# Causal attention and a gated two-layer network on one core: every matmul with 128 columns of weights written as two of 64

## The chip, the cores and the metric

One NeuronCore of one Trainium2 chip (trn2) runs the whole kernel. The metric is device time of one execution in microseconds (us), on one core. PE is TensorE (matmuls; PEld is its weight loads), DVE is VectorE, ACT is ScalarE, POOL is GpSimd, and SP is the engine that issues the DMAs. [...]

## The reference

```python
# q, k, v: (4 batches, 12 heads, 448 positions, 64)   w_in: 768 x 2048   w_out: 2048 x 768
scores = (q @ k^T) / sqrt(64);  mask above the diagonal with -1e9
attn = exp(scores - rowmax);  attn = attn / (rowsum + 1e-9)
x = (attn @ v) as 1792 tokens x 768
h = x @ w_in
g = h * sigmoid(1.702 * h)
out = g @ w_out          # 1792 x 768, float32
```

The result has to be close to float32, so most operands are held as a pair of float16 tensors, a high part and a rest, and each product is three matmuls: high by high, high by rest, rest by high. The first attention batch does its scores in float32 instead. The weights arrive as 64-bit words and are rebuilt as float32 on chip.

## The kernel before, in words

**Tiling.** Each batch of 448 positions is cut into two blocks, of 256 and of 192 positions, so there are eight blocks. In a block, heads go two at a time; one such pair of heads is a *unit* (six per block, 48 in all). The work on PE comes in kinds:

- `turn` (matmul on line 870) transposes float32 q and k by an identity, two matmuls of 64 weight columns at a time (first batch only).
- `scores_of` makes scores: in the first batch `scores32` (line 1060), one float32 matmul with 128 weight columns per 64 queries of two heads; otherwise `scores` (line 1068), float16, where the two heads are two matmuls of 64 weight columns that write partitions 0 to 63 and 64 to 127 of one PSUM tile.
- `pv` in `unit` (line 1197) multiplies probabilities by v, also as pairs of 64 columns, 12 pairs in a unit of the 192-wide blocks (nine of them with 192 moving columns, three with 64).
- `h_slice` (line 1268) is x by w_in: 2304 matmuls with 128 columns of weights, 256 or 192 moving columns, nine to a step of the order. I call it H below.
- `out_tile` (line 1333) is g by w_out, 384 moving columns, six to a step; I call it O. Its weights are 128 columns of `gT`. The ring `gT` has seven places of 64 tokens, so in two of the 14 token tiles the 128 columns lie apart, and there the kernel already uses pairs of 64 (`takes`).
- `gram` (line 621, the columns' products of a piece of weights or v, 128 by 128, for a bound on its size) and `all_max` (line 430, one maximum brought to all partitions) are small matmuls with 128 columns.

In this text a matmul with 64 columns of weights is *narrow*, one with 128 is *wide*; two narrow ones that follow each other on the two halves of the array are a *pair*.

**What sets the order of the work.** Nothing is issued in program order. Each step is put on a list with `Ops.add` (costs per engine, what it reads and writes, a priority, how long its DMA takes, and whether its matmuls are narrow). `Ops.order` then searches: `forward` lays the steps out on the five engines by priority, `backward` makes new priorities from that layout, `late` scores a layout, and the best of 300 rounds is issued. In this ordering clock a change between narrow and wide on PE costs `SWITCH`, and `forward` has two PE queues, `PE` and `PE64`: it stays with the kind it has unless the other kind is ahead in priority by more than `keep`, drawn from `KEEP` for each round:

```python
SWITCH = 0.093
same, other = (ready["PE64"], q) if mode else (q, ready["PE64"])
q = same if same and (not other or same[0][0] <= other[0][0] + keep) else other
```

A DMA in the ordering clock starts `DMA_START` after its issue, holds the bus for its `dma`, and lands `DMA_END` later; transposes take `ROWS` for each 128 rows.

Of the kernel before, what the change touches and what calls it, by code (L numbers as in the profile page):

```python
# [59 lines left out]
class Ops:  # L60
# [11 lines left out]
    LOAD = 0.68  # L72
    DMA_START, DMA_END, DMA_DEPTH = 1.0, 0.8, 8
    ROWS = 0.19

# [8 lines left out]

    def add(self, costs, fn, r=(), w=(), prio=0.0, dma=0.0, narrow=False):
        deps = set()
        for key in r:
            if key in self.wrote:
                deps.add(self.wrote[key])
        for key in w:  # L90
            if key in self.wrote:
                deps.add(self.wrote[key])
            deps.update(self.read.get(key, ()))
        me = len(self.ops)
        for key in r:
            self.read.setdefault(key, []).append(me)
        for key in w:
            self.wrote[key] = me
            self.read[key] = []
        deps.discard(me)  # L100
        self.ops.append((costs, fn, sorted(deps), prio, dma, narrow))

    ROUNDS, STEPS, SPREAD, KEEP = 300, 6, (0.0, 0.0, 1.0, 3.0, 8.0), (0.0, 1.5, 4.0)

    SWITCH = 0.093

    def order(self):
        rnd = Random(SEED)
        best = now = self.scored([o[3] for o in self.ops], 0.0)
        bad = 0  # L110
        for _ in range(self.ROUNDS):
            spread = rnd.choice(self.SPREAD)
            now = self.scored(self.backward(now, spread, rnd), rnd.choice(self.KEEP))
# [9 lines left out]
    def scored(self, prios, keep):  # L123

        result, fin, last = self.forward(prios, keep)
        return 0.5 * last + sum(0.25 * self.late(result, Random(x)) for x in (1, 2)), result, fin

    def late(self, result, rnd):
        free = dict.fromkeys(self.ENGINES, 0.0)
        end = [0.0] * len(self.ops)  # L130
        bus, flying, clock, mode = 0.0, [], Clock(), False
        for i, e in result:
            costs, _, deps, _, dma, narrow = self.ops[i]
            start = max([free[e]] + [end[d] + self.HOP for d in deps])
            if e == "SP":
                start = max([start] + flying[-self.DMA_DEPTH :][: len(flying) // self.DMA_DEPTH][:1])
                free[e] = start + costs[e]
                bus = max(bus, start + self.DMA_START) + dma
                end[i] = bus + self.DMA_END + 0.8 * rnd.random()
                flying.append(end[i])  # L140
                continue
            if e == "PE":
                end[i] = clock.after(start, costs[e] + (self.SWITCH if narrow != mode else 0.0))
                mode = narrow
            else:
                end[i] = start + costs[e] * (1 + 0.03 * rnd.random()) + (0.15 * rnd.random() if e == "POOL" else 0.0)
            free[e] = end[i]
        return max(free.values())

    def backward(self, found, spread, rnd):  # L150
        _, result, fin = found
# [12 lines left out]
        while done < n:  # L164
# [4 lines left out]
            for e in self.ENGINES:  # L169
                if free[e] > now + 1e-9 or not ready[e]:  # L170
                    continue
                _, i = heappop(ready[e])
                costs, _, deps, _, dma, _ = self.ops[i]
                left[i] = free[e] = now + costs[e]
# [17 lines left out]

    def forward(self, prios, keep):

# [3 lines left out]
        for i, o in enumerate(self.ops):  # L198
            for d in o[2]:
                after[d].append(i)  # L200
        ready = {e: [] for e in self.ENGINES + ("BULK", "PE64")}
        mode = False
        coming = [(0.0, i) for i in range(n) if not wait[i]]
        taken = [None] * n
        free = dict.fromkeys(self.ENGINES + ("BULK", "PE64"), 0.0)
        bus = 0.0
# [5 lines left out]
        while len(result) < n:  # L212
            while coming and coming[0][0] <= now + 1e-9:
                _, i = heappop(coming)
                for e in self.ops[i][0]:
                    late = self.SECOND if e != next(iter(self.ops[i][0])) else 0.0
                    kind = "BULK" if e == "SP" and self.ops[i][4] > 1.0 else "PE64" if self.ops[i][5] else e
                    heappush(ready[kind], (prios[i] + late, i))
            moved = False
            free["BULK"] = max(free["SP"], bus - TUNE["slack"])  # L220
            for e in ("BULK",) + self.ENGINES:
                q = ready[e]
                if e == "PE":
                    same, other = (ready["PE64"], q) if mode else (q, ready["PE64"])
                    q = same if same and (not other or same[0][0] <= other[0][0] + keep) else other
                while q and taken[q[0][1]] is not None:
# [6 lines left out]
                e = "SP" if e == "BULK" else e  # L233
                costs, _, _, _, dma, narrow = self.ops[i]
                taken[i] = e
                free[e] = end = now + costs[e]
                if e == "PE":
                    end = clock.after(now, costs[e] + (self.SWITCH if narrow != mode else 0.0))
                    free[e] = free["PE64"] = end
                    mode = narrow  # L240
                if e == "SP":
# [80 lines left out]
def kernel(  # L322
# [9 lines left out]
    nc = tc.nc  # L332
# [79 lines left out]
    def flip(e, dst, src):  # L412
# [3 lines left out]
        )  # L416

    def all_max(src, src_key, tag, turn, prio):

# [5 lines left out]
        else:  # L425
# [3 lines left out]
            {"PE": 0.1},  # L429
            lambda e: nc.tensor.matmul(row, top, one16, start=True, stop=True),  # L430
            [src_key, "one16"], row_keys, prio,
# [181 lines left out]
    def gram(x, keys, ps, ps_key, first, last, prio):  # L613
# [5 lines left out]
        def mm(e):  # L619
            for k, m in blocks:  # L620
                nc.tensor.matmul(
                    ps[:, :P], t[:, k, m], t[:, k, m],
                    start=first and (k, m) == blocks[0],
                    stop=last and (k, m) == blocks[-1],
                )
# [148 lines left out]
    def v_batch(b, prio):  # L774
        st = bst[b]
        for j in range(NJ):
# [5 lines left out]
                ),  # L782
                [], [("vraw", j, 0)] + ([("vraw", j, 1)] if r == P else []), prio, dma=2.18 * r / P,
            )
# [77 lines left out]
    def turn(src, r, keys, prio):  # L862
# [10 lines left out]

        add({"PE": 2 * (4 * r / 2.4 + 210) / 1e3}, mm, keys + ident_keys, [("T", h)], prio, narrow=True)
        return ps_t[:, 256 * h : 256 * h + 2 * r].rearrange("p (t x) -> p x t", t=2), ("T", h)

    def k_unit32(u, c0, c1, prio):
# [5 lines left out]
        keys = [("q16", m, j) for j in range(4)]  # L883
        load_heads(f, k[0, 2 * u : 2 * u + 2, 64 * c0 : 64 * c1], r, [keys[:2], keys[2:]], prio, 0.045 * (c1 - c0))
        got, got_key = turn(f, r, keys, prio)
# [8 lines left out]
    def q_unit32(n, u, prio):  # L894
# [5 lines left out]
        keys = [("qf", i, j) for j in range(2)]  # L900
        load_heads(f, q[b, 2 * u : 2 * u + 2, 64 * c0 : 64 * c1], r, [[x] for x in keys], prio, 0.045 * ni)
        got, got_key = turn(f, r, keys, prio)
# [65 lines left out]
    def q_pair(n, u, prio):  # L968
# [7 lines left out]
        for a in range(2):  # L976
            for j in range(2):
# [6 lines left out]
                    ),  # L984
                    [], keys[-1:], prio, dma=0.09 * ni,
                )
# [61 lines left out]
    def scores_of(n, u, run, qt, qt_key, prio):  # L1048
# [9 lines left out]
        def scores32(e):  # L1058
            for i, ps in zip(run, places):
                nc.tensor.matmul(  # L1060
                    ps, qt[:, i - c0].rearrange("p j w -> p (j w)"), kt[:, : 64 * (i + 1)], start=True, stop=True
                )

# [14 lines left out]
        else:  # L1078
            add(
                {"PE": 2 * (o / 2.4 + 17 * len(run)) / 1e3}, scores, [qt_key] + kt_keys, bank(sb), prio, narrow=True  # L1080
            )
# [52 lines left out]
    def unit(n, u, prio):  # L1134
# [59 lines left out]
        def pv(e):  # L1194
# [11 lines left out]
            {"PE": sum((64 * (c1 - t[1]) / 2.4 + 5) for t in terms) / 1e3}, pv, v_keys + all_keys, [("PV", vb)], prio,  # L1206
            narrow=True,
        )
# [45 lines left out]
    def h_slice(n, sl, prio):  # L1254
# [7 lines left out]
        for t in range(2):  # L1262
            for a in range(0, NU, half):

                def mm(e, a=a, t=t):
                    for u in range(a, a + half):
                        for gw, gx in ((0, 0), (0, 1), (1, 0)):
                            nc.tensor.matmul(  # L1268
                                ph[:, t],
                                wib[:, sl, u, gw, t * P : (t + 1) * P],  # L1270
                                xT[x][:, gx, u, :w],
                                start=(u == 0 and gw + gx == 0),
                                stop=(u == NU - 1 and gw == 1),
                            )
# [32 lines left out]
    def out_tile(tt, prio):  # L1307
# [4 lines left out]

        takes = [(rs[0], P, 0)] if rs[1] == rs[0] + 1 else [(r, 64, 64 * j) for j, r in enumerate(rs)]
        for nh in range(2):
# [12 lines left out]
            for f0 in range(0, NFC, 2):  # L1327

                def mm(e, f0=f0, po=po, nh=nh):
                    for f in range(f0, f0 + 2):  # L1330
                        for gg, gw in ((0, 0), (0, 1), (1, 0)):
                            for r, m, o in takes:
                                nc.tensor.matmul(  # L1333
                                    po[o : o + m, :OH],
                                    gT[:, f, gg, 64 * r : 64 * r + m],
                                    wo_pair(f, gw, nh),
# [8 lines left out]
                    + [("gT", r, f, g) for f in (f0, f0 + 1) for g in range(2) for r in rs],  # L1345
                    [("O", pb)] + ([] if pb else [("T", 0), ("T", 1)]), 1e6 + prio, narrow=len(takes) > 1,
                )
# [114 lines left out]
```

## Time and profile before

| what | value |
|---|---|
| median of 3 runs | 640.23 us |
| the three runs | 640.47, 640.23, 637.7 us |
| span of the profiled execution, first to last instruction | 633.9 us |
| own time of the profiled execution | not listed apart; its span is 6.3 us under the median, 3.8 us under the fastest run |
| PE busy | 582.6 us, 92% of the span, 5723 matmuls |
| DVE busy | 422.4 us, 67% |
| ACT busy | 357.2 us, 56% |
| POOL busy | 96.6 us, 15% |

The slices of the span matter more than the totals: the share of an engine over the whole kernel is a mean over a start, in which weights and inputs arrive and are rebuilt, and a long rest. Matmuls are pipelined: a row's mean duration (246 to 327 ns) is that of one matmul from entry to modelled end, and their spacing, which is what one costs in a row of them, is read from how long a run of them took by the timeline or the chain.

### The profile page before, as it was taken

The numbers are of one execution on the slowest core, as the hardware profiler recorded it, in microseconds if no ns is written. First come the engines' busy times: TensorE is split into PE (matmuls) and PEld (weight loads), VectorE is DVE, ScalarE is ACT, GpSimd is POOL, SyncE is SP. The second block draws the span as 40 slices with busy tenths as digits, with TensorE's granted clock in tenths as the row PEclk, the third lists the DMA queues.
The fourth block names the chain that finished last, engine by engine and source line by source line (L and its number), as shares of the span: only waits on it lengthen the run. The fifth ranks groups of instructions, "written<-read, shape, count | busy, mean of one in ns | idle before, by whom it ended". The sixth has DMA issues, their size and how long they took to land. (4 is left out here: it accounts for less than half of the span.)

```text
span 633.9 us, 14759 instructions
## 1 busy us (share of the span) xinstructions
PE 582.6 (92%) x5723; PEld 439.5 (69%) x5723; DVE 422.4 (67%) x1128; ACT 357.2 (56%) x835; POOL 96.6 (15%) x235
## 2 busy tenths in 40 slices
PE   4777688978999999998999999999999999999997
PEld 3555466754588767876678667885679688777964
DVE  4999899999978898977498976769644213101300
ACT  4878888778657776758465565557343223012210
POOL 2233220043202124121021521001000000000000
PEclk9976689999999999999999999999999999999999
DMA  8999969678599687999847798627620040000000
GB/s 276 271 277 293 220 224 284 194 188 166 110 176 190 120 164 124 180 159 173 176 103 135 136 181 160 127 62 130 122 67 2 13 96 1 3 26 26 1 26 26
DMA packets 226407, 85.71 MB, mean 135 GB/s; under 512 B 207137, under 2 KB 216097, under 8 KB 226337
## 3 DMA queue, kind: packets, MB, share of 16 engines
q1 hardware_dynamic: 226336, 84.76, 62.7%
q8 instruction: 45, 0.74, 0.5%
q14 instruction: 26, 0.20, 0.1%
HBM read 41.68 MB, written 5.51 MB: 74 GB/s over the span
## 5 line engine op out<-in xcount | busy, mean ns | idle before, releaser
L1268 PE MATMUL ps_h<-xT,wib 128*128 128x192 f16 (+1 forms) x2304 | 239.3, 261 | 3.5 <-DVE gT L481 3.4
L1333 PE MATMUL ps_o<-wob,gT 128*128 128x384 f16 (+1 forms) x1536 | 233.8, 326 | 5.3 <-DVE wob L481 2.3
L1268 PEld LDWEIGHTS <-wib 128*128 128x128 f16 x2304 | 207.0, 98 | 31.8 <-issue 12.1
L1333 PEld LDWEIGHTS <-gT 128*128 128x128 f16 (+1 forms) x1536 | 131.4, 101 | 87.0 <-issue 12.6
L1105 ACT ACTIVATE z<-z,cols 128x320 f32<-128x320 f32 (+5 forms) x168 | 83.8, 500 | 47.1 <-DVE cols L1091 40.1
L1294 DVE SCALAR_TENSOR_TENSOR ps_h<-t,ps_h 128x512 f32<-128x512 f32 (+1 forms) x64 | 39.9, 624 | 76.5 <-ACT t L1289 76.3
L481 DVE SCALAR_TENSOR_TENSOR p<-z,cols,p 128x384 f16<-128x384 f32 (+3 forms) x168 | 82.6, 523 | 3.0 <-ACT p L476 1.9
L1091 DVE CUSTOM_DVE_ANT_0 z<-ps_s,mask,cols 128x384 f32<-128x384 f32 (+6 forms) x126 | 55.8, 478 | 30.1 <-PE ps_s L1068 30.1
L1289 ACT ACTIVATE t<-ps_h,cols 128x512 f32<-128x512 f32 (+1 forms) x64 | 40.1, 627 | 60.0 <-PE ps_h L1268 59.5
L476 ACT ACTIVATE p<-z,cols 128x128 f16<-128x128 f32 (+3 forms) x108 | 55.3, 538 | 15.4 <-DVE cols L1169 6.7
L1163 POOL TENSOR_SCALAR cols<-cols 128x2 f32<-128x2 f32 (+1 forms) x70 | 20.1, 287 | 208.6 <-ACT z L1105 207.7
L481 DVE SCALAR_TENSOR_TENSOR gT<-ps_h,gT 128x512 f16<-128x512 f32 (+1 forms) x64 | 39.6, 620 | 15.8 <-ACT gT L476 15.7
L476 ACT ACTIVATE gT<-ps_h 128x512 f16<-128x512 f32 (+1 forms) x58 | 31.1, 539 | 28.3 <-DVE ps_h L1294 28.1
L476 ACT ACTIVATE ob<-ps_o,cols 128x384 f32<-128x384 f32 x23 | 13.2, 575 | 59.8 <-PE ps_o L1333 59.8
L1197 PEld LDWEIGHTS <-v 128*64 128x64 f16 x864 | 38.4, 113 | 9.6 <-issue 7.6
L1197 PE MATMUL ps_v<-PT,v 128*64 128x192 f16 (+3 forms) x864 | 41.1, 243 | 4.1 <-DMA PT<-p 4.1
L1068 PE MATMUL ps_s<-kT,qT 128*64 128x192 f16 (+4 forms) x504 | 38.8, 277 | 2.4 <-DVE cols L1091 1.3
L1060 PE MATMUL ps_s<-kT,qT 128*128 128x64 f32 (+6 forms) x84 | 29.3, 468 | 2.6 <-DVE cols L1091 1.9
L1024 POOL TENSOR_SCALAR q<-q 128x512 f16<-128x512 f16 (+1 forms) x30 | 25.2, 841 | 43.0 <-ACT q L476 30.1
L1105 ACT ACTIVATION_READ_ACCUMULATOR z<-z,cols 128x1 f32 x168 | 31.7, 188 | 0.0
L476 ACT ACTIVATE wob<-wob 128x768 f32<-128x768 f32 (+1 forms) x19 | 20.8, 1095 | 15.6 <-DMA wob<-in_moe_w_in_dram 10.6
L1068 PEld LDWEIGHTS <-qT 128*64 128x64 f16 x504 | 19.6, 110 | 13.9 <-issue 9.9
(89 smaller groups left out, 541.1 us busy)
## 6 DMA issues: line engine op xcount, KB each, us to landing
wob<-in_moe_w_in_dram SPq DMA_DIRECT2D x16, 768.0 KB, 6.0
wob<-in_moe_w_out_dram SPq DMA_DIRECT2D x9, 768.0 KB, 5.5
vraw<-in_moe_w_out_dram SPq DMA_DIRECT2D x7, 768.0 KB, 5.4
out_dram<-ob SPq DMA_DIRECT2D x28, 192.0 KB, 2.1
vraw<-in_v_dram SPq DMA_DIRECT2D x12, 384.0 KB, 5.7
kf<-in_k_dram SPq DMA_DIRECT2D x36, 112.0 KB, 2.9
qf<-in_q_dram SPq DMA_DIRECT2D x48, 64.0 KB, 3.2
qf<-in_q_dram SPq DMA_DIRECT2D x48, 48.0 KB, 2.7
```

What stands on the lines that cost most here:

```text
L476: nc.scalar.activation(out=dst, in_=src, func=AF.Copy, scale=sc)
L481: nc.vector.scalar_tensor_tensor(out=dst, in0=src, scalar=sc, in1=hi, op0=ALU.mult, op1=ALU.subtract)
L1024: nc.gpsimd.tensor_scalar(out=dst, in0=src, scalar1=1.0, scalar2=1.0, op0=ALU.mult, op1=ALU.mult)
L1060: nc.tensor.matmul(ps, qt[:, i - c0].rearrange("p j w -> p (j w)"), kt[:, : 64 * (i + 1)], start=True, stop=True)
L1068: nc.tensor.matmul(ps[64 * j : 64 * j + 64], qt[:, g, i - c0, 64 * j : 64 * j + 64], kt[:, : i + 1, 64 * j : 64 * j + 64], start=(g == 0), ...
L1091: lambda e: nc.vector.tensor_tensor_reduce(out=z[:, :w], in0=ps, in1=mask[:, S - w :], scale=c, scalar=3.0e38, op0=ALU.add, op1=ALU.min, a ...
L1105: lambda e: nc.scalar.activation(out=z[:, :w], in_=z[:, :w], func=AF.Exp, bias=m, scale=-1.0, accum_out=l),
L1197: nc.tensor.matmul(ps[64 * j : 64 * j + 64, 64 * (first - c0) : w], vt[:, gv, J, j, :], PT[pi][:, at, gp, 64 * j : 64 * j + 64], start=(t ...
L1268: nc.tensor.matmul(ph[:, t], wib[:, sl, u, gw, t * P : (t + 1) * P], xT[x][:, gx, u, :w], start=(u == 0 and gw + gx == 0), stop=(u == NU - ...
L1289: lambda e: nc.scalar.activation(out=th, in_=ph, func=AF.Tanh, scale=ts[:, sl : sl + 1]),
L1294: lambda e: nc.vector.scalar_tensor_tensor(out=ph, in0=th, scalar=1.0, in1=ph, op0=ALU.add, op1=ALU.mult),
L1333: nc.tensor.matmul(po[o : o + m, :OH], gT[:, f, gg, 64 * r : 64 * r + m], wo_pair(f, gw, nh), start=(f == 0 and gg + gw == 0), stop=(f == ...
```

## The change

A helper `halves` issues a matmul with 128 weight columns as two with 64, for output partitions 0 to 63 and 64 to 127, with the same moving operand. `gram`, `all_max`, `scores32` and `h_slice` use it, and `out_tile` always takes its pairs of 64. So no matmul is wide any more. The flag `narrow`, the price `SWITCH`, the second PE queue and `keep` leave the ordering clock. Its DMA constants are set to other values: start 1.23 for 1.0, end 0.95 for 0.8, transposes 0.214 for 0.19 per 128 rows, and some loads' durations. The order is searched anew with these.

```diff
-    DMA_START, DMA_END, DMA_DEPTH = 1.0, 0.8, 8
-    ROWS = 0.19
+    DMA_START, DMA_END, DMA_DEPTH = 1.23, 0.95, 8
+    ROWS = 0.214
...
-    ROUNDS, STEPS, SPREAD, KEEP = 300, 6, (0.0, 0.0, 1.0, 3.0, 8.0), (0.0, 1.5, 4.0)
-
-    SWITCH = 0.093
+    ROUNDS, STEPS, SPREAD = 300, 6, (0.0, 0.0, 1.0, 3.0, 8.0)
...
-                if e == "PE":
-                    same, other = (ready["PE64"], q) if mode else (q, ready["PE64"])
-                    q = same if same and (not other or same[0][0] <= other[0][0] + keep) else other
...
+    def halves(out, lhsT, rhs, start, stop):
+
+        for o in range(0, P, 64):
+            nc.tensor.matmul(out[o : o + 64], lhsT[:, o : o + 64], rhs, start=start, stop=stop)
+
...
-                nc.tensor.matmul(
-                    ps, qt[:, i - c0].rearrange("p j w -> p (j w)"), kt[:, : 64 * (i + 1)], start=True, stop=True
-                )
+                halves(ps, qt[:, i - c0].rearrange("p j w -> p (j w)"), kt[:, : 64 * (i + 1)], True, True)
...
-                            nc.tensor.matmul(
+                            halves(
                                 ph[:, t],
                                 wib[:, sl, u, gw, t * P : (t + 1) * P],
                                 xT[x][:, gx, u, :w],
-                                start=(u == 0 and gw + gx == 0),
-                                stop=(u == NU - 1 and gw == 1),
+                                u == 0 and gw + gx == 0,
+                                u == NU - 1 and gw == 1,
                             )
...
-        takes = [(rs[0], P, 0)] if rs[1] == rs[0] + 1 else [(r, 64, 64 * j) for j, r in enumerate(rs)]
...
-                            for r, m, o in takes:
+                            for j, r in enumerate(rs):
                                 nc.tensor.matmul(
-                                    po[o : o + m, :OH],
-                                    gT[:, f, gg, 64 * r : 64 * r + m],
+                                    po[64 * j : 64 * j + 64, :OH],
+                                    gT[:, f, gg, 64 * r : 64 * r + 64],
```

How the instructions move, at two places. First PE, where a step of O (tile `ps_o`, weights `gT`) meets the `pv` of a unit (tile `ps_v`, probabilities `PT`, weights `v`); the size is weight columns by moving columns. Before:

```order
L1333 LDWEIGHTS gT
L1333 MATMUL ps_o_98<-wob,gT 128x384
L1197 LDWEIGHTS v_71
L1197 MATMUL ps_v<-PT_79,v_71 64x192
L1197 LDWEIGHTS v_71
L1197 MATMUL ps_v<-PT_79,v_71 64x192
```

And in the changed kernel, where the `pv` of a unit ends and O goes on:

```order
L1191 LDWEIGHTS v_72
L1191 MATMUL ps_v<-PT_80,v_72 64x64
L1325 LDWEIGHTS gT
L1325 MATMUL ps_o_98<-wob,gT 64x384
L1325 LDWEIGHTS gT
L1325 MATMUL ps_o_98<-wob,gT 64x384
```

The matmul with 128 columns became two of 64, each with its own weight load. In all PE has 10962 rows before and 18352 now. Over the whole order the matmuls change between 128 and 64 columns 129 times before and never now. Before, the `pv` of two units stands together four times, as 48 matmuls; now each of the 48 units stands by itself.

Second, SP's queue at the start, where the loads of w_in (into `wob`) stand among those of q and k for the float32 units. Before:

```order
L652 DMA wob<-in_moe_w_in_dram 128x3x512 x2
L856 DMA q_76<-in_k_dram 128x128 x2
L856 DMA qf<-in_q_dram 128x128 x2
L856 DMA q_76<-in_k_dram 128x128
L856 DMA qf<-in_q_dram 128x128
L856 DMA q_76<-in_k_dram 128x128
L652 DMA wob<-in_moe_w_in_dram 128x3x512
```

Now:

```order
L648 DMA wob<-in_moe_w_in_dram 128x3x512 x2
L852 DMA q_76<-in_k_dram 128x128 x2
L852 DMA qf<-in_q_dram 128x128 x2
L648 DMA wob<-in_moe_w_in_dram 128x3x512 x2
L852 DMA q_76<-in_k_dram 128x128 x2
L852 DMA qf<-in_q_dram 128x128 x2
L648 DMA wob<-in_moe_w_in_dram 128x3x512
```

The second slice of w_in moved ahead of the second unit's k and q.

## Rows read from the trace of the kernel before

**Rows 1.** The page, parts 1 and 2: busy times, then slices of the span

```profile
span 633.9 us, 14759 instructions
...
PE 582.6 (92%) x5723; PEld 439.5 (69%) x5723; DVE 422.4 (67%) x1128; ACT 357.2 (56%) x835; POOL 96.6 (15%) x235
...
PE   4777688978999999998999999999999999999997
...
DVE  4999899999978898977498976769644213101300
...

```

**Rows 2.** Busy time in two stretches: stretch, its length, then each engine's busy time

```profile
core 0: us, PE busy (x) PEld busy (x) DVE busy (x) ACT busy (x) POOL busy (x), PEclk, DMA share, GB/s
0.00:120.00 120.00, 87.35 (x731) 66.89 (x732) 104.63 (x242) 94.54 (x189) 28.17 (x63) 0.87 1.00 265
120.00:634.00 514.00, 495.30 (x4994) 372.56 (x4993) 317.77 (x886) 262.69 (x647) 68.46 (x172) 1.00 0.55 105
```

**Rows 3.** PE's waits, 120 to 634: awaited operation, total us, times, longest

```profile
PE ps_o L1333 <- DVE wob L481: 2.3, 4, 1.0
...
PE ps_h L1268 <- DVE gT L481: 2.3, 3, 1.4
...
PE ps_v L1197 <- DMA PT<-p: 1.2, 2, 0.8
...
PE ps_o L1333 <- DVE gT L481: 0.2, 1, 0.2
```

**Rows 4.** The chain that ended last: start us, us, what, and matmuls

```profile
504.36 0.98 PE ps_h L1268 x9
505.34 0.97 PE ps_o L1333 x6
506.31 0.98 PE ps_h L1268 x9
507.30 0.97 PE ps_o L1333 x6
...
599.60 0.74 PE ps_h L1268 x9
...
604.01 26.34 PE ps_o L1333 x162
```

**Rows 5.** PE's timeline, three stretches: start us, us (last matmul's end included), group

```profile
129.25 1.15 PE L1268 MATMUL ps_h<-xT,wib 128*128 128x256 f16 x9
130.33 1.86 PE L1197 MATMUL ps_v<-PT,v 128*64 128x192 f16 x48
132.12 1.15 PE L1333 MATMUL ps_o<-wob,gT 128*128 128x384 f16 x6
...
179.35 0.75 PE L1068 MATMUL ps_s<-kT,qT 128*64 128x64 f16 x16
179.93 1.84 PE L1197 MATMUL ps_v<-PT,v 128*64 128x192 f16 x48
181.70 1.15 PE L1333 MATMUL ps_o<-wob,gT 128*128 128x384 f16 x6
...
536.55 1.17 PE L1333 MATMUL ps_o<-wob,gT 128*64 128x384 f16 x12
537.64 5.09 PE L1268 MATMUL ps_h<-xT,wib 128*128 128x256 f16 x45
542.66 11.89 PE L1333 MATMUL ps_o<-wob,gT 128*64 128x384 f16 x144
554.49 5.11 PE L1268 MATMUL ps_h<-xT,wib 128*128 128x256 f16 x54
```

**Rows 6.** PE's weight loads by form: busy us, mean ns of one

```profile
L1268 PEld LDWEIGHTS <-wib 128*128 128x128 f16 x2304 | 207.0, 98 | 31.8 <-issue 12.1
...
L1197 PEld LDWEIGHTS <-v 128*64 128x64 f16 x864 | 38.4, 113 | 9.6 <-issue 7.6
...
L1060 PEld LDWEIGHTS ps_s<-kT,qT 128*128 128x128 f32 x84 | 15.7, 235 | 5.3 <-DVE cols L1091 2.5 <-issue 1.1 <-ACT qT L476 0.9
...
L870 PEld LDWEIGHTS ps_o<-ident,q 128*64 128x64 f32 x48 | 4.1, 190 | 10.6 <-issue 8.6 <-DMA q<-in_k_dram 1.0 <-ACT kT L476 0.9
```

**Rows 7.** DMA queues of the page: packets, MB, share of 16 engines

```profile
q1 hardware_dynamic: 226336, 84.76, 62.7%
q8 instruction: 45, 0.74, 0.5%
```

More of the change, by code (lines that the diff above doesn't have):

```diff
@@ L100, in add @@
         deps.discard(me)
-        self.ops.append((costs, fn, sorted(deps), prio, dma, narrow))
-    ROUNDS, STEPS, SPREAD, KEEP = 300, 6, (0.0, 0.0, 1.0, 3.0, 8.0), (0.0, 1.5, 4.0)
-    SWITCH = 0.093
+        self.ops.append((costs, fn, sorted(deps), prio, dma))
+    ROUNDS, STEPS, SPREAD = 300, 6, (0.0, 0.0, 1.0, 3.0, 8.0)
     def order(self):
         rnd = Random(SEED)
-        best = now = self.scored([o[3] for o in self.ops], 0.0)
+        best = now = self.scored([o[3] for o in self.ops])
         bad = 0
@@ L130, in late @@
         end = [0.0] * len(self.ops)
[L131 removed]
+        bus, flying, clock = 0.0, [], Clock()
         for i, e in result:
[L133 removed]
+            costs, _, deps, _, dma = self.ops[i]
             start = max([free[e]] + [end[d] + self.HOP for d in deps])
@@ L142, in late @@
             if e == "PE":
-                end[i] = clock.after(start, costs[e] + (self.SWITCH if narrow != mode else 0.0))
-                mode = narrow
+                end[i] = clock.after(start, costs[e])
             else:
@@ L233, in forward @@
                 e = "SP" if e == "BULK" else e
-                costs, _, _, _, dma, narrow = self.ops[i]
+                costs, _, _, _, dma = self.ops[i]
                 taken[i] = e
@@ L237, in forward @@
                 if e == "PE":
-                    end = clock.after(now, costs[e] + (self.SWITCH if narrow != mode else 0.0))
-                    free[e] = free["PE64"] = end
-                    mode = narrow
+                    free[e] = end = clock.after(now, costs[e])
                 if e == "SP":
@@ L429, in all_max @@
             {"PE": 0.1},
-            lambda e: nc.tensor.matmul(row, top, one16, start=True, stop=True),
+            lambda e: halves(row, top, one16, True, True),
             [src_key, "one16"], row_keys, prio,
@@ L1079, in scores_of @@
             add(
-                {"PE": 2 * (o / 2.4 + 17 * len(run)) / 1e3}, scores, [qt_key] + kt_keys, bank(sb), prio, narrow=True
+                {"PE": 2 * (o / 2.4 + 17 * len(run)) / 1e3}, scores, [qt_key] + kt_keys, bank(sb), prio
             )
@@ L1267, in mm @@
                         for gw, gx in ((0, 0), (0, 1), (1, 0)):
-                            nc.tensor.matmul(
+                            halves(
                                 ph[:, t],
```

36 lines of the change are left out of this document (17 added, 19 removed).

## The prediction

> **What bounds the kernel now.** I read the page first. PE is busy 92% of the 633.9 us span, and its slices say where the rest is: from the eighth slice (about 125 us) on they are nines, before it they are fours to eights, while DVE's are nines [rows 1]. Two stretches make that sharper. Up to 120 us PE works 87.35 us of 120 and DVE 104.63; from 120 us PE works 495.30 of 514, DVE 318 and ACT 263 [rows 2]. So the start belongs to DVE, the loads and the half clock (granted mean 0.87), and PE has 32.65 us of idle time in it. After it PE is the bound. Its waits there are twelve lines of at most 2.3 us, 25 waits and 16.1 us in all, on DVE, on ACT and on transposes [rows 3]. A microsecond taken from PE after 120 us is therefore worth nearly a microsecond. One taken before is worth little.
>
> Next, what PE's time after 120 us consists of. The chain gives the pace of wide matmuls when PE waits for nothing: nine H with 256 columns in 0.98 us (0.109 each), nine with 192 in 0.74 (0.082 each), six O in 0.97, and 162 O in 26.34 us, 0.1626 each [rows 4]. H and O alternate there without extra time, so a change of tile or weights costs nothing. A change of width does. In the timeline nine H before a `pv` take from 129.25 to 130.33, 1.08 us where 0.98 is usual; twelve narrow O take 1.09 us where the six wide ones take 0.97; 45 H take 5.02 us (537.64 to 542.66) where 45 times 0.109 is 4.90; 72 pairs of O take 11.83 us where 72 times 0.1626 is 11.71 [rows 5]. Each such stretch holds one change of width and is 0.10 to 0.12 us too long. I take 0.10, since the times have two decimals and the longer stretches may hold a slower pair as well.
>
> **The change part by part.**
>
> *Changes of width go.* The order has 129 before and none now. Along the timeline 33 lie before 120 us and 96 after it. After: 96 x 0.10 = 9.6 us off (11.5 at 0.12). Before: 3.3 us, which I count at nothing, because 32.65 us of idle time lie beside them [rows 2]. Were PE the bound there, they would be a further gain.
>
> *One wide matmul becomes a pair.* The two write different halves of the partitions and stream the same moving operand. If they ran one after the other, H would double: 1152 x (0.109 + 0.082) = 220 us more, and O about as much. The kernel already has such pairs, and they run together: 144 narrow O, 72 pairs, take 11.83 us with one change of width in it, so 11.73 / 72 = 0.1629 us a pair against 0.1626 for a wide one [rows 4, 5]. For 192 columns, 48 `pv` matmuls are 18 pairs of 192 columns and six of 64; 130.33 to 132.12 less one change leaves 1.69 us. At H's 0.082 the 18 take 1.48, which leaves 0.035 for each of the six, above their share by columns (0.027). If all the excess were in the 18, a pair would take 0.085, 0.003 more than H. So the cost lies between nothing and 0.003 us a pair for 2304 H (6.9 us), and about 0.0003 for 1152 wide O (0.3 us). I take the long run's 0.0003 for all 3456, 1.0 us, because that run is the one nearest to a steady stream; 256 columns lie between the two widths seen.
>
> *Twice the instructions.* PE's rows go from 10962 to 18352. A 192-wide pair is two loads and two matmuls in 0.082 us, 20.6 ns each. The densest stretch of before is 16 score and 48 `pv` matmuls, 128 instructions with their loads, from 179.35 to 181.70: 18.4 ns each, the change at the end included [rows 5]. So the rate needed has been held for 128 instructions, though for no longer. Nothing added. The fetch of instructions (45 packets, 0.74 MB, 0.5% of the DMA engines [rows 7]) grows by 18352 / 10962 to about 75 packets and 0.8%, and no wait of PE after 120 us names it: nothing. [...]
>
> *Float32 scores, `gram`, `all_max`.* The 84 float32 matmuls load 128 columns in a mean of 235 ns, where the narrow float32 of `turn` loads 64 in 190 [rows 6]. If the loads set the pace, pairs would gain 84 x 0.045 = 3.8 us; if two loads ran in series, they would lose 84 x 0.145 = 12 us. Since narrow pairs overlap their loads elsewhere and these mostly stand in the start where PE has idle time, I take nothing and keep both ends. `gram` and `all_max` are pairs of 128 columns, between widths already seen: nothing.
>
> *The order is new.* With no price on width, `pv` of single units, scores and H are mixed freely. All PE work is the same in columns. What can change is how often PE waits. When PE goes faster, DVE's results come relatively later. Some 58 of the 96 changes lie before 360 us, where DVE's slices are still mostly eights and nines [rows 1], so at worst 5.8 us of the gain turn into waits there, at best none. I take a quarter, 1.5 us; the row nearest is that PE idles only some 16 us in 514 with DVE that full, so DVE is not the bound yet. In SP's queue a w_in slice goes ahead of the second unit's k and q. At the start PE's idle time bounds what this gives or takes, and I put it at nothing with several microseconds to either side.
>
> *Sum.* 633.9 - 9.6 + 1.0 + 1.5 = 626.8 us of span. The page doesn't list the own time of the profiled execution; its span is 6.3 us under the median of the runs, and I carry that over: 633.1, so **633 us**, 1.1% less. A measurement here tells about 0.5%, 3.2 us, from no change.
>
> [...] The 64-column loads have means of 110 to 113 ns as against 98 for 128 columns [rows 6], yet 48 of them pass in 1.79 us with their matmuls, 37 ns each [rows 5]; they overlap. [...]
>
> **The rivals.**
>
> 1. *No change that can be measured.* The time that PE saves becomes waits on DVE, or the new search lands in an order that is a little worse. For: DVE's nines up to 340 us. Against: PE has H and O in stock and hardly waits. All of the 5.8 us before 360 us lost, and 2 us more: a span of 633.9 - 9.6 + 1.0 + 7.8 = 633.1, a time of 639 us.
> 2. *Slower, because a stream of pairs is paced by its instructions or weight loads.* Place: H with 192 columns, where four instructions have 82 ns. It decides from 20.6 ns an instruction on, and eats the whole gain at 9.6 us / 2304, 4 ns a pair. What long stretches of before prove is only H's own pace, two instructions in 82 ns, 41 ns each [rows 4]. At that upper bound 192-wide pairs take 164 ns and 256-wide ones too: 1152 x (0.082 + 0.055) = 158 us more, 791 us. [...] Against it: 128 instructions at 18.4 ns [rows 5].
> 3. *Slower, because the start loses.* The first 120 us hold 32.65 us of PE idle time and the half clock; if the new sequence of loads and transposes makes PE's supply late by half as much again, 16 us are added: 633 + 16 = 649. It decides from about 13 us. For: every queue is rearranged. Against: the planner weighs the same steps with DMA times that are longer, so loads are issued earlier rather than later.
> 4. *Faster than forecast.* The start gains 5 us of its idle time by the same token, and the price is 0.12: 626.
>
> That the change doesn't do what it says can be left out: the order has no wide matmul left, and the row of alternating H and O shows that no price hangs on anything but the width.
>
> **How the numbers follow.** Forecast (627 to 638 us): 0.65. Rival 1: 0.17. Rival 2: 0.05. Rival 3: 0.07. Rival 4: 0.06. Under 637.0 us is the forecast but for a little, and rival 4: faster 0.69. Rival 1 and the forecast's upper edge: same 0.18. Rivals 2, 3 and the tail of 1: slower 0.13. The range goes from 621, rival 4 with the 3.3 us of changes before 120 us gained as well and rounding to spare, to 645, which takes in rival 1, the 6.9 us bound on pairs and the lighter half of rival 3; outside are rival 2 and the rest of 3, about one in ten, and what I can't name on the lower side.
>
> **What would show it.** Right: no group of wide matmuls; 18 pairs (36 matmuls) of H with 192 columns in 1.48 us and 12 O in 0.97 to 0.98; neighbours S, `pv`, H and O in the timeline with no 0.1 us between them; PE busy after 120 us about 9 us less and its waits there under 20 us. Wrong: nine pairs of H in more than 0.76 us (rival 2); waits after 120 us of 25 us or more, on DVE above all (rival 1); fewer PE-busy microseconds in the first 120 us (rival 3). A granted clock under 1.00 after 120 us would be a cause that I don't expect: through the 11.83 us of narrow O it stays in the nines [rows 1].

## The result, and the profile after

The changed kernel takes 617.07 us (median of 4 runs, 616.13 to 618.26), the kernel before 639.23 beside it (4 runs, 637.7 to 640.47). The ratio is 0.9671, 95% interval 0.9635 to 0.9706: 3.3% faster. Forecast were 633 us and, at the lowest, 621. The direction was right, the size was not: three times the gain forecast.

First the page of the changed kernel: busy times, then three of its rows by slices. PE has 9502 matmuls and as many weight loads, where it had 5723 of each; its busy time falls from 582.6 to 566.6 us [rows 1]. PEclk is the clock granted to TensorE as a share of its full clock, in tenths in the slices. At its lower level it reads 0.50, as in every 2 us from 46 to 56 us of this trace and of that of the kernel before; that is the half clock of this text.

```profile
span 614.9 us, 22331 instructions
...
PE 566.6 (92%) x9502; PEld 503.8 (82%) x9502; DVE 419.9 (68%) x1117; ACT 359.5 (58%) x830; POOL 95.3 (16%) x251
...
PE   4667689888999999999998999999999999999997
...
DVE  4999999998978789996588885886685213102300
...
PEclk9786899999999999999999999999999999999999
```

The profiled execution of the changed kernel took 616.57 us with a span of 614.9, so 1.7 us lie around a span. Every later run of the kernel before that lists its span has 1.7 to 1.8 us there. The span of 633.9 that I worked from thus belongs to an execution of some 635.6 us, and the 6.3 us that I carried over between span and median were mostly the spread of that kernel's runs. Span against span, the change is 19.0 us; the forecast of the span was 626.8, so 11.9 us were missed there.

Busy time of the changed kernel in the two stretches that stand in [rows 2], with the columns named in the first line:

```profile
core 0: us, PE busy (x) PEld busy (x) DVE busy (x) ACT busy (x) POOL busy (x), PEclk, DMA share, GB/s
0.00:120.00 120.00, 85.58 (x1262) 69.89 (x1264) 110.07 (x260) 96.31 (x185) 25.02 (x66) 0.87 1.03 268
120.00:615.00 495.00, 481.01 (x8246) 433.95 (x8240) 309.85 (x859) 263.14 (x645) 70.31 (x185) 1.00 0.61 109
```

After 120 us PE is busy 14.3 us less (495.30 to 481.01) and idle 4.7 us less (18.7 to 14.0). Its waits there, the counterpart of [rows 3], are 16 waits of 9.9 us in all; before they were 16.1 us, in 23 waits (not 25, as I had counted). All nine lines:

```profile
PE ps_s L1062 <- DVE cols L1085: 3.2, 5, 1.7
PE ps_o L1325 <- DVE wob L477: 2.1, 3, 0.7
PE ps_o L412 <- DVE wob L599: 1.0, 1, 1.0
PE ps_o L1325 <- ACT wob L472: 1.0, 1, 1.0
PE ps_s L412 <- DVE cols L1085: 0.8, 2, 0.4
PE ps_o L1325 <- DVE ob L474: 0.7, 1, 0.7
PE ps_s L1062 <- DVE cols L628: 0.5, 1, 0.5
PE ps_h L412 <- DVE xT L477: 0.4, 1, 0.4
PE ps_s L1062 <- DMA qT<-q: 0.2, 1, 0.2
```

The pace of pairs is read from long stretches of the changed kernel's chain (start us, us, what, matmuls), the counterpart of [rows 4]:

```profile
495.65 27.51 PE ps_h L412 x504
...
527.07 27.30 PE ps_o L1325 x336
...
557.81 20.79 PE ps_h L412 x504
578.60 0.97 PE ps_o L1325 x12
579.57 0.74 PE ps_h L412 x18
```

A pair of H with 256 columns takes 27.51 / 252 = 0.1092 us, of O 27.30 / 168 = 0.1625, of H with 192 columns 20.79 / 252 = 0.0825. The wide matmuls took 0.109, 0.1626 and 0.082, so pairs are as fast to within 0.0005 us. The last stretch holds 1008 instructions at 20.6 ns each. In these three streams the time goes with the moving columns alone, 0.42 to 0.43 ns for each.

The work that is done by 120 us also grew: 217 H before, and 472 narrow ones now, 236 pairs, so 19 more, worth 2.1 us at 0.109 us each. The `pv` of one more unit is done by then too (96 matmuls for 72), some 0.8 us.

So the 19.0 us of span can be put together. Both spans are cut at 120 us, so all of it shows after that. PE's idle time gives 4.7. Of the 14.3 us of busy time the 96 changes of width make about 10 (at 0.104 us, by e1 below) and the work that now lies before 120 us 2.9; 1.4 us are left without a name.

### The profile page after: what moved, and what is told of

It reads as the page before. It is cut to its first block, busy times and chain, and to the rows that moved or that the text cites. A ratio compares the mean times of both kernels' runs of the same rounds, so it can differ in the third digit from the quotient of the medians.

```text
span 614.9 us, 22331 instructions
## 1 busy us (share of the span) xinstructions
PE 566.6 (92%) x9502; PEld 503.8 (82%) x9502; DVE 419.9 (68%) x1117; ACT 359.5 (58%) x830; POOL 95.3 (16%) x251
## 4 chain that ended last, share of the span: by engine, by line
PE 55%; DVE 13%; ACT 4%; issue 3%; DMA 3%; POOL 2%; SPq 1%; DVEq 0%; ACTq 0%; POOLq 0%
PE ps_o L1325 25%; PE ps_h L412 25%; PE ps_v L1191 3%; PE ps_s L1062 3%; DVE p L477 2%; DMA qf<-in_q_dram 2%; DVE z L1085 2%; ACT z L1099 1%; DVE wob L477 1%; POOL cols L1227 1%; DVE ps_h L1287 1%; DVE p L474 1%; SPq L977 1%; DVE wob L599 1%; ACT waste L462 1%
## 5 line engine op out<-in xcount | busy, mean ns | idle before, releaser
L412 PE MATMUL ps_h<-xT,wib 128*64 128x256 f16 (+1 forms) x4608 | 239.7, 259 | 1.5 <-DVE gT L477 0.9
L1325 PE MATMUL ps_o<-wob,gT 128*64 128x384 f16 x2688 | 237.5, 326 | 3.8 <-DVE wob L477 2.1
L412 PEld LDWEIGHTS <-wib 128*64 128x64 f16 x4608 | 225.4, 110 | 6.7 <-issue 3.5
L1325 PEld LDWEIGHTS <-gT 128*64 128x64 f16 x2688 | 177.2, 110 | 39.1 <-issue 7.1
L1085 DVE CUSTOM_DVE_ANT_0 z<-ps_s,mask,cols 128x192 f32<-128x192 f32 (+5 forms) x126 | 55.9, 476 | 14.0 <-PE ps_s L1062 13.5
L472 ACT ACTIVATE p<-z,cols 128x256 f16<-128x256 f32 (+3 forms) x101 | 52.7, 554 | 15.6 <-DVE cols L1163 12.2
L472 ACT ACTIVATE gT<-ps_h 128x384 f16<-128x384 f32 (+1 forms) x57 | 30.7, 538 | 25.0 <-DVE ps_h L1287 25.0
L1062 PE MATMUL ps_s<-kT,qT 128*64 128x64 f16 (+4 forms) x504 | 39.5, 273 | 3.9 <-DVE cols L1085 3.2
L412 PE MATMUL ps_s<-kT,qT 128*64 128x128 f32 (+6 forms) x168 | 29.9, 476 | 4.8 <-DVE cols L1085 3.4
L1062 PEld LDWEIGHTS <-qT 128*64 128x64 f16 x504 | 24.6, 110 | 7.3 <-issue 4.8
L412 PE MATMUL ps_o<-wob 128*64 128x128 bf16 x384 | 18.4, 244 | 8.8 <-DVE wob L599 5.1
L474 DVE TENSOR_SCALAR p<-z,cols 128x128 f16<-128x128 f32 (+2 forms) x67 | 25.7, 408 | 1.0
```

The lines of the kernel that those rows point to most:

```text
L412: nc.tensor.matmul(out[o : o + 64], lhsT[:, o : o + 64], rhs, start=start, stop=stop)
L472: nc.scalar.activation(out=dst, in_=src, func=AF.Copy, scale=sc)
L474: nc.vector.tensor_scalar(out=dst, in0=src, scalar1=sc, scalar2=None, op0=ALU.mult)
L1062: nc.tensor.matmul(ps[64 * j : 64 * j + 64], qt[:, g, i - c0, 64 * j : 64 * j + 64], kt[:, : i + 1, 64 * j : 64 * j + 64], start=(g == 0), ...
L1085: lambda e: nc.vector.tensor_tensor_reduce(out=z[:, :w], in0=ps, in1=mask[:, S - w :], scale=c, scalar=3.0e38, op0=ALU.add, op1=ALU.min, a ...
L1325: nc.tensor.matmul(po[64 * j : 64 * j + 64, :OH], gT[:, f, gg, 64 * r : 64 * r + 64], wo_pair(f, gw, nh), start=(f == 0 and gg + gw == 0), ...
```

## The experiments

The kernel before had medians of 635.0 to 639.2 us beside the different sets of runs, so what is compared below is each kernel's ratio to it, with its interval. I name the parts of the change **pairs** (narrow matmuls), **price** (the ordering clock's price on a change of width, with its two queues) and **DMA constants**. A first set of four takes them apart.

### e1: the changed kernel's order, wide matmuls

```diff
     def halves(out, lhsT, rhs, start, stop):
-        for o in range(0, P, 64):
-            nc.tensor.matmul(out[o : o + 64], lhsT[:, o : o + 64], rhs, start=start, stop=stop)
+        nc.tensor.matmul(out, lhsT, rhs, start=start, stop=stop)
...
+        takes = [(rs[0], P, 0)] if rs[1] == rs[0] + 1 else [(r, 64, 64 * j) for j, r in enumerate(rs)]
```

> The changed kernel's order, step for step, with its matmuls written wide again: 243 changes of width in the order where the changed kernel has none and the kernel before has 129. Theory A (a change of width costs 0.094 to 0.100 us of PE time wherever PE is the bound; the rest of the gain is the order): 190 or so of the 243 lie after 120 us and cost 18 us, so 617 + 18 = 635 us, up to 640 if the early ones count too. Rival B (the pairs themselves are faster, and the price of a change is small): between 620 and 630 us.

Measured: 633.04 us, ratio 0.995 (0.9929 to 0.997). The same order is 15.3 us of span slower with wide matmuls (630.2 to 614.9). Its busy time in the two stretches:

```profile
0.00:120.00 120.00, 87.07 (x772) 66.05 (x773) 109.76 (x258) 96.05 (x185) 23.95 (x65) 0.89 1.03 268
120.00:630.00 510.00, 501.78 (x4954) 364.56 (x4951) 310.96 (x860) 264.32 (x645) 70.91 (x187) 1.00 0.57 105
```

After 120 us PE is busy 501.78 us for 481.01: 20.8 us for the 200 changes of width that its timeline has there, 0.104 us each, at a granted clock of 1.00 in both. That is the price read from the kernel before. But PE's waits there are only 4.7 us, in five lines, where the changed kernel has 9.9. So taking the changes away returned 20.8 us and 5 to 6 of them became waits. Theory A holds with that correction; its 635 to 640 us were too high because it left out the waits.

### e2: the old order, pairs

```diff
-                            nc.tensor.matmul(
+                            halves(
                                 ph[:, t],
...
-                            for r, m, o in takes:
+                            for r, m, o in [(r, 64, 64 * j) for j, r in enumerate(rs)]:
```

The same edit stands in `gram`, `all_max` and `scores32`; the planner still counts wide and narrow as it did, so every step stands where it stood.

> The order of the kernel before, step for step, with every matmul written as a pair: no change of width is left. Theory A: the 96 changes after 120 us go, 9 to 10 us, and the waits of PE stay about as they were (16 us after 120 us): 639 - 9 = 630 us, span about 624. Rival B (the pairs by themselves give the whole gain): 617 to 620 us. Rival C (the DMA constants and the free order give nothing, and waits shrink by themselves once PE's changes go): 622 to 626 us.

Measured: 639.47 us, ratio 1.0057 (1.0026 to 1.0087). All three expectations failed: the 96 changes of width are gone and the kernel is not faster, but a little slower. Its busy time after 120 us and its page's clock say where the gain went:

```profile
0.00:120.00 120.00, 82.94 (x1194) 66.67 (x1194) 104.07 (x239) 93.07 (x186) 28.75 (x63) 0.89 0.99 258
120.00:640.00 520.00, 491.40 (x8308) 444.68 (x8308) 319.64 (x890) 264.20 (x649) 66.93 (x172) 0.99 0.57 106
```

PE idles 28.6 us of 520 for 18.7 of 514 before; its listed waits went from 16.1 to 24.6 us. The longest lines:

```profile
PE ps_h L421 <- DVE gT L486: 4.8, 3, 2.5
PE ps_v L1200 <- DMA PT<-p: 4.4, 3, 2.0
PE ps_o L421 <- DVE cols L637: 3.9, 2, 3.5
```

The longest of them, 3.5 us, can be followed in the timeline (start us, us, instruction; in brackets the idle time before it and what ended it):

```profile
119.03 0.56 PE L421 MATMUL ps_o<-wob 128*64 128x128 bf16 x12
...
119.39 0.53 PE L875 MATMUL ps_o<-ident,qf 96*64 96x96 f32 x8
...
120.22 0.88 ACT L481 ACTIVATE wob<-wob 128x768 f32<-128x768 f32 x1 [2.26 <-DMA wob<-in_moe_w_out_dram]
...
122.54 0.60 DVE L583 TENSOR_SCALAR wob<-wob 128x768 uint16<-128x768 uint16 x1 [2.10 <-DMA wob<-in_moe_w_out_dram]
123.04 0.28 DVE L637 TENSOR_REDUCE cols<-ps_o 128x1 f32<-128x128 f32 x1
...
123.37 0.25 PE L421 MATMUL ps_o<-one,cols 128*64 128x128 bf16 x2 [3.46 <-DVE cols L637]
```

DVE stands 2.10 us before its piece of w_out has landed. The small maximum on `ps_o` (L637) stands behind that piece in DVE's queue, though the `gram` that wrote `ps_o` ended at 119.6, and PE stands behind the maximum. After this wait the granted clock falls to half, and it does so twice more, behind PE's waits of 2.5 us (on `gT`, L486) and 2.1 us (on `cols`, L1094). The stretches of e2 (in all four the clock of the kernel before is 1.00):

```profile
120.00:140.00 20.00, 16.30 (x296) 14.72 (x298) 17.20 (x34) 17.10 (x28) 3.39 (x8) 0.91 0.64 181
...
180.00:200.00 20.00, 16.17 (x338) 15.31 (x336) 14.08 (x48) 10.12 (x29) 2.35 (x8) 0.97 0.92 167
200.00:220.00 20.00, 20.00 (x427) 19.58 (x425) 14.47 (x49) 14.80 (x48) 1.44 (x6) 0.94 0.89 143
...
240.00:260.00 20.00, 17.91 (x298) 17.20 (x296) 16.87 (x49) 12.58 (x29) 8.22 (x20) 0.92 0.77 140
```

What the half clock costs is seen in the start of the kernel before, where it holds for 3.4 us (0.66 from 85 to 85.5 us, 0.50 up to 88.5, 0.92 up to 89, then 1.00): 27 wide H take 4.61 us there (85.20 to 89.81), 1.67 more than at the pace of 0.109, which is about half of the 3.4. In e2 27 pairs of H, the first of them 0.1 us behind the wait of 3.5 us, take 4.62 us (123.45 to 128.07). In all PE runs 10.2 us at half clock there (10.4 by the rounded means above) and is busy throughout, which costs it 5.1 us. That closes the account: its busy time falls by 3.9 us only, and 3.9 + 5.1 = 9.0 us for 96 changes, 0.094 each. The idle time takes 9.9 us back, and the clock 5.1. Not every such wait is followed by a fall: PE of the changed kernel stands 2.4 us at 114 us and keeps its clock (1.00 from 112 to 120 us), and PE of e2 stands 2.0 us at 334 us and keeps it (9 tenths in that slice of its page). No run took the clock's fall away by itself. So in this order, made for a slower PE, the faster one waited more, and behind three of its waits it lost clock as well.

### e3 and e4: the DMA constants apart

e3 is the changed kernel with the old constants, e4 the kernel before with the new ones; the edit is the same, in opposite directions (for e3):

```diff
-    DMA_START, DMA_END, DMA_DEPTH = 1.23, 0.95, 8
-    ROWS = 0.214
+    DMA_START, DMA_END, DMA_DEPTH = 1.0, 0.8, 8
+    ROWS = 0.19
...
-        load_heads(f, k[0, 2 * u : 2 * u + 2, 64 * c0 : 64 * c1], r, [keys[:2], keys[2:]], prio, 0.062 * (c1 - c0))
+        load_heads(f, k[0, 2 * u : 2 * u + 2, 64 * c0 : 64 * c1], r, [keys[:2], keys[2:]], prio, 0.045 * (c1 - c0))
```

> The changed kernel with the old DMA constants in the ordering clock; pairs and a search without the price on width. Theory A1 (freedom from the price on width makes the better order): 615 to 620 us, as the changed kernel. Theory A2 (the DMA constants make the better order): 625 to 630 us, with waits of PE after 120 us of 15 us or more.

> The kernel before with only the DMA constants of the ordering clock changed; wide matmuls, the price on width and both PE queues kept (149 changes of width in its order, 129 before). Theory A1: 636 to 642 us, no change that can be measured. Theory A2 (the DMA constants make the better order): 628 to 633 us with PE's waits after 120 us near 10 us.

Measured: e3 635.01 us, ratio 0.998 (0.9959 to 1.0001); e4 628.44 us, ratio 0.9885 (0.9859 to 0.9911). Theory A2 has the direction in both, though e3 lies 5 us above its range: pairs with a free search but the old constants gain nothing clear of noise, and the constants alone gain 1.2%, with wide matmuls and more changes of width than before. In e3 PE waits 22.2 us after 120 us. ACT's waits on DMAs there, by line (total us, times, longest):

```profile
ACT waste L462 <- DMA qf<-in_q_dram: 13.9, 12, 4.1
ACT q L472 <- DMA qT<-q: 12.3, 7, 3.1
```

In the changed kernel the same two are

```profile
ACT waste L462 <- DMA qf<-in_q_dram: 8.0, 6, 2.6
...
ACT q L472 <- DMA qT<-q: 0.4, 1, 0.4
```

All of ACT's waits on DMAs after 120 us are 37.7 us in e3 and 11.8 in the changed kernel. The transfers themselves are no faster: from issue to landing the page has 3.3 and 2.9 us for the two sizes of q in e3, 3.2 and 3.1 in the changed kernel. So it is the order that moved, of the loads and of those who use them.

### A second seed, and e4's order in pairs

The search draws random numbers, so one order could be luck. Three kernels were repeated with `SEED = 1` for 2, and with them e5: e4's planner and order, its matmuls written as pairs.

> The kernel before with another seed of the search for the order (1 for 2). Theory D (the DMA constants make the better orders): 632 to 642 us. Theory L (a search's result is luck of 5 us or more either way): anywhere between 625 and 645 us, as likely near 628 as near 636.

> Pairs, no price on width, old DMA constants, seed 1 for 2. Theory D: 630 to 637 us, 12 us or more over the changed kernel at the same seed. Theory L: as likely as not within 5 us of the changed kernel at the same seed.

> The changed kernel with seed 1 for 2. Theory D: 615 to 622 us. Theory L: 617 was a lucky order, and this lies between 620 and 630 us.

> The order of e4 (the planner of before with its price on width and both queues, and the new DMA constants), step for step, with every matmul a pair: 149 changes of width become none, 112 of them after 120 us. Theory P (taking the changes away pays where the order leaves PE few waits; e4 has 6.8 us of them after 120 us): 628 - 112 x 0.096 + 3 to 5 us of new waits = 620 to 622 us. Rival Q (taking the changes away turns into waits, as with the old order in e2): 627 to 631 us, waits after 120 us of 15 us or more. Rival R (the price on width must go from the planner too, or the order stays worse): above 622 us with few waits.

Measured: before 635.88 us, ratio 1.0018 (0.9985 to 1.0051); pairs with old constants 632.72, ratio 0.9951 (0.9922 to 0.9981); the changed kernel 621.22, ratio 0.9784 (0.9732 to 0.9836). e5 took 624.74 us, ratio 0.9834 (0.9799 to 0.987). Theory D (the constants) holds at the second seed: 11.5 us between old and new constants with pairs, a little under the 12 it asked for. Theory L has its part as well: the changed kernel is 4 us slower at this seed, 1.1% by the ratios.

e5 against e4 is the second case of an order held while its changes of width go. The stretch after 120 us of e4, then of e5:

```profile
120.00:628.00 508.00, 498.42 (x5003) 374.75 (x5003) 311.46 (x869) 267.86 (x658) 66.96 (x180) 0.99 0.56 106
```

```profile
120.00:624.00 504.00, 487.93 (x8326) 443.41 (x8326) 311.24 (x868) 267.58 (x658) 68.02 (x180) 1.00 0.59 107
```

PE's busy time falls by 10.5 us for 112 changes of width, and its idle time up to the end of each span (628.2 and 623.5) grows from 9.8 to 15.6, its listed waits from 6.8 to 13.1. The 10.5 us aren't all changes of width. Behind a wait of 2.23 us e4 runs at half clock for 6.8 us (0.83 in the mean of 20 us), and six O take 2.13 us, about twice the 1.14 that they take in e5, which waits 2.02 us there and keeps its clock (1.00). The stretch in e4, then in e5, and one step of O in each:

```profile
140.00:160.00 20.00, 17.14 (x99) 9.98 (x98) 18.12 (x48) 16.60 (x38) 4.47 (x15) 0.83 0.66 125
146.29 2.13 PE L1333 MATMUL ps_o<-wob,gT 128*128 128x384 f16 x6
```

```profile
140.00:160.00 20.00, 16.20 (x200) 10.59 (x195) 19.25 (x54) 17.71 (x41) 6.30 (x17) 1.00 0.71 136
146.23 1.14 PE L1336 MATMUL ps_o<-wob,gT 128*64 128x384 f16 x12
```

PE is busy for 6.2 us of that half clock, so it makes 3.1 us of the 10.5 and leaves 7.4, which is 0.066 us a change. After 450 us, where PE waits in neither kernel, the last 20 changes take 2.0 us, 0.10 each; why those between take less stays open. Theory P had the mechanism; it rated the new waits too low, at 3 to 5 us, and didn't see the clock. Its range was missed by 3 us. What the price in the planner costs on top is 624.74 less 617.07, some 8 us (10 by the ratios) on one pair of kernels; against the changed kernel at its other seeds it is 3 to 4 us by the ratios, so it isn't clear of the seed.

### Which constants, and how far

> The changed kernel, whose ordering clock has only the new start and end of a DMA (1.23 and 0.95 for 1.0 and 0.8); transposes' rows and the loads' durations are the old ones. The parts of 18 us between e3 (635 us, all old) and the changed kernel (617 us, all new): if every load lands late by the missing 0.38 us and that is what PE waits for in the end, 618 to 622 us and ACT's waits on DMAs after 120 us near 12 us; if it is the durations that are too short, 630 to 635 us and ACT's waits on DMAs above 25 us.

> The other half: new durations of transposes and loads, old start and end of a DMA. If the durations are what matters 618 to 622 us; if the 0.38 us of start and end matter, 628 to 635 us. If both halves give about half, 624 to 628 us each.

> The changed kernel with the same step in the DMA constants made once more (start 1.46, end 1.10, rows 0.238, loads longer by as much again). If the gain is only that DMA work is no longer expected too early, more of it gives little or nothing: 615 to 620 us, PE's waits after 120 us between 5 and 10 us. If any margin is good, 610 to 614 us. If the true values matter and too long is as bad as too short, 625 us and up.

> e4 (wide matmuls, price on width in the planner, new DMA constants) at seed 1, beside the kernel before at seed 1 (635.9 us). Theory D (the DMA constants make the better orders): 626 to 631 us. Theory L (e4's 8 us were luck): 633 us or more.

Measured: f1 (start and end) 624.53 us, ratio 0.9832 (0.979 to 0.9874); f2 (durations) 622.71, ratio 0.9803 (0.9749 to 0.9858); f3 (the step made twice) 624.2, ratio 0.9827 (0.977 to 0.9884); e4 at seed 1 629.88, ratio 0.9881 (0.9807 to 0.9955). Each half of the constants gives a good part, and neither is the one cause; f2 and f3 fell between the ranges that I had set. The last confirms e4: with wide matmuls it is 6 us below the kernel before at the same seed (9 by the ratios, 0.9881 and 1.0018). f3 gives no sign that more is better. The two stretches of f1, then of f3:

```profile
0.00:120.00 120.00, 85.98 (x1336) 71.45 (x1338) 108.59 (x249) 100.63 (x200) 34.60 (x69) 0.90 1.05 276
120.00:623.00 503.00, 480.89 (x8170) 436.88 (x8166) 314.00 (x867) 259.43 (x640) 67.72 (x174) 1.00 0.58 106
```

```profile
0.00:120.00 120.00, 79.04 (x1114) 63.21 (x1116) 101.15 (x243) 91.90 (x183) 30.22 (x63) 0.83 0.96 260
120.00:621.00 501.00, 488.73 (x8394) 448.26 (x8390) 332.11 (x926) 260.45 (x640) 58.09 (x145) 1.00 0.61 110
```

f1 has the better start (85.98 us of PE work at a clock of 0.90, 500 narrow H by 120 us) and the worse rest: PE idles 22.1 us after 120 us. f3 has the worse start (79.04 us at 0.83, 326 narrow H) and a rest with 12.3 us idle. That suggests that short constants let the rest wait and long ones hold up the start, on one order each. For the rest there is more: in kernels without a wide matmul and with a free search, PE's idle time after 120 us is 21 to 26 us wherever the loads' durations are the old ones (e3, its second seed, g1 of the next set, f1), and 10 to 14 wherever they are the new ones or longer (the changed kernel at three seeds, g2, f2, f3). So fewer waits go with the durations, not with start and end. For the start it isn't shown: the changed kernel has 236, 216 and 198 pairs of H done by 120 us at its three seeds, and with the old constants it is 197 to 207; f1's 250 and f3's 163 are the two ends. My expectation that ACT's waits on DMAs would tell the good orders apart fell: f1 has 36.3 us of them and f3 5.5, at the same time.

### More search, another seed

> Pairs, no price on width, old DMA constants, as e3, with 1200 rounds of search for 300. If the constants mislead the search, more of it doesn't help: 628 to 636 us, ACT's waits on DMAs after 120 us above 25 us. If e3's order was only an unlucky search: 615 to 623 us.

> The changed kernel with 1200 rounds of search for 300. If the score that the search lowers is near the chip's time: 611 to 617 us. If its last microseconds are below what the ordering clock knows: 616 to 623 us.

> The changed kernel with seed 3 for 2. With 617 and 621 us at seeds 2 and 1, 615 to 625 us; above 628 would say that the result of the change hangs on the seed as much as on the constants.

Measured: g1 633.73 us, ratio 0.9945 (0.9914 to 0.9975); g2 616.35 us, ratio 0.9672 (0.9644 to 0.97); g3 622.36 us, ratio 0.9766 (0.9711 to 0.9821). Four times the search doesn't mend the old constants and doesn't improve on the new ones beyond the noise (0.9672 and 0.9671). At three seeds the changed kernel has ratios of 0.967, 0.978 and 0.977. So e3's order isn't an unlucky search; with the new values about 1% is left to chance, and the changed kernel's seed is the luckiest of the three. No version here beats the changed kernel. That the new values are better because they are nearer to the chip's own times is not shown: no run compares them, and f3, longer still, is no better.

The parts don't simply add. At seed 2, the changed kernel's own, the constants give 1.2% with wide matmuls and 3.1% with pairs and a free search; at seed 1 they give 1.4 and 1.7%, so that the large joint gain at seed 2 is in part its seed.

## Why the prediction was right or wrong

*What bounds the kernel.* Right in the trace of before: PE after 120 us, the start before. It is also why the gain is there at all.

*Changes of width, 9.6 us off at 0.10 each.* Right. With the order held it is 0.104 us of PE's busy time for each in e1, and 0.094 in e2 once the half clock is counted; e4 and e5 give less, 0.066, and 0.10 where nothing waits. That they count as nothing before 120 us fits: with the order held, the H done by 120 us are 233 and 236 (e1 and the changed kernel, 43 changes before 120 us), 217 and 216 (before and e2, 33), 207 and 207 (e4 and e5, 37).

*Pairs, +1.0 us.* The bound was right, and the value is its lower end: nothing. The 0.0003 us a pair hung on taking 0.10 us for the change of width in the long run of O; at 0.13 nothing is left of it.

*Twice the instructions, +0.* Right; 1008 instructions ran at 20.6 ns each, and the fetch of instructions is 74 packets and 0.8% of the DMA engines, as forecast. Rival 2 is refuted: a 192-wide pair takes 82.5 ns, though the 64-column loads of these pairs read 110 ns each. Two of them one after the other would be 220 ns by that mean, so in these pairs the loads overlap.

*Float32 scores, `gram`, `all_max`, nothing.* Right to about 1 us: in the same order the scores' tiles keep PE busy 72.35 us with wide float32 matmuls (e1) and 72.00 with pairs, and `gram` on the weights 17.2 and 18.4. Neither the gain of 3.8 us nor the loss of 12 came.

*The order is new, +1.5 us.* This is the step that failed, by size and by sign. I named the new DMA constants in the change and gave them no term of their own. In its place the runs showed that the order made with them is a gain, and the larger of the two parts at either seed: 18 us with pairs at one seed and 11.5 at another, 8 and 6 us with wide matmuls. Pairs and the free search without them give 1 us in e3 and 3 at seed 1. In the account of the span the new order took 4.7 us of PE's idle time after 120 us away, where I had added 1.5, and did some 2.9 us more of PE's work by 120 us, where I had put nothing.

*PE's savings become waits: a quarter of 5.8 us, the same 1.5.* The mechanism was right where the order is held, and too small: 5 to 6 us of 20.8 in e1, a quarter of the whole and not only of the part before 360 us, about 6 of 10.5 in e5, and 9.9 us in e2, all of it. The half clock behind the waits, 5.1 us in e2, wasn't foreseen. That the changed kernel has fewer waits than the kernel before goes with its new order, and there with the loads' durations; without them (e3) it has more, 22.2 us for 16.1.

*The carry from span to median, 6.3 us.* Wrong: 1.7 us lie around a span. The rest was the spread of runs, and put 4.6 us on the forecast.

*Luck.* At seeds 1 and 3 the same change gives 2.2 and 2.3%, which is 625 us beside a kernel before of 639 and within the range of 621 to 645. So about 1% of the miss is the luck of the changed kernel's seed. The sign of the term isn't: PE's idle time after 120 us is 14.0, 12.8 and 13.4 us at the three seeds, and 18.7 and 16.6 us before at two.

*The rivals.* Rival 1 (the gain becomes waits) is what e2 and e3 show, which lack the constants; the kernel as it stands isn't it. Rival 4 (the start gains 5 us) had the right direction: the start gained about 3. What it lacked is the rest of the gain, after 120 us.

## What to carry to other kernels

Before a price is put on a new order, ask what the planner now believes: other durations in it can be worth as much as the work that is saved, as they were here, and a saving on the bounding engine can turn into waits, all of it in e2, if the order isn't made anew around it. Run more than one seed of such a search before a difference of 1% is believed. Hold the order and change the instructions, then hold the instructions and change the order; neither alone told here what both did. Here a pair of 64-column matmuls took what one of 128 took at 192, 256 and 384 moving columns (0.0825, 0.1092 and 0.1625 us for 0.082, 0.109 and 0.1626), and writing all of them narrow removed 0.07 to 0.10 us of PE's time at each change of width (0.066 in e5, 0.094 in e2, 0.104 in e1) for nothing but instructions.

## What the runs showed of the hardware that was not expected

The same PE program less its 96 late changes of width ran slower (e2, ratio 1.0057), with 9.9 us more of idle time and 5.1 us lost to half clock behind three waits of 2.1 to 3.5 us. The pairs themselves lose nothing in e2, whose last 162 pairs of O take the 26.34 us of the 162 wide ones before [rows 4], so the slowing is in waits and the clock. Two waits at the same place of the same order, 2.23 us in e4 and 2.02 in e5, ended once with a fall of the granted clock and once without (0.83 and 1.00 from 140 to 160 us). And 64-column loads with a mean of 110 ns sustain one load and one matmul every 41 ns for 20.79 us, so the mean duration of a load in the trace is not its pace.
